# Background matmuls as four column tiles, and one more quad of VectorE exps in the slots of chunks four and five

## The chip, the cores and the metric

The kernel runs on one core of a Trainium2 chip. Five engines work side by side: TensorE (matmuls; PE in the profile, its weight loads PEld), VectorE (DVE), ScalarE (ACT), GpSimd (POOL) and SyncE (SP, which issues the transfers here). The metric is the device time of one execution in microseconds, as the median of several runs; lower is better.

## What is computed

A transformer block for 2048 tokens of 640 features: attention of 32 heads of 20 features after a layer norm, then a gated MLP of 1728 hidden features after another one, each with its residual. All inputs and the output are bfloat16.

```python
def reference(A_x, A_wqkv, A_wo, B_x, B_w_gate, B_w_up, B_w_down):
    def _A_ref(x, wqkv, wo):
        ...
        scores = jnp.einsum("bhqd,bhkd->bhqk", q, k) * (Dh ** -0.5)
        p = _softmax(scores, axis=-1)
        o = jnp.einsum("bhqk,bhkd->bhqd", p, v)
        return (lambda x, *d: x.transpose(*d))(o, 0, 2, 1, 3).reshape(B, S, D) @ wo
    def _B_ref(x, w_gate, w_up, w_down):
        ...
        h = _gelu(g) * u
        return jnp.einsum("bsf,fd->bsd", h, w_down)
    x = A_x
    h = x + _A_ref(_layernorm(x, axis=-1), A_wqkv, A_wo)
    h2 = h + _B_ref(_layernorm(h, axis=-1), B_w_gate, B_w_up, B_w_down)
    return h2
```

`B_x` is not used.

## The kernel before

**Chunks, slots, tiles.** The queries are cut into seven chunks of 512, 512, 256, 256, 256, 128 and 128 rows (`CHUNKS`; chunks four and five are indices 3 and 4). Four heads make a group; a slot is one chunk with so many groups that its accumulator fills 512 columns (1, 2 or 4 groups), which gives 32 slots: 8, 8, 4, 4, 4, 2, 2. A slot has 64 tiles. A tile is the scores of one head for 128 keys in its partitions and 512 columns (a 256-row chunk puts two blocks of keys in a tile, a 128-row chunk four).

**Attention.** A unit (`unit`) is three or two tiles, in turn in the PSUM banks 0 to 2 and 3 to 4. Its score matmuls (L919) use the array as four row tiles of 32 rows, one per head; then one ScalarE activation takes the exp of the whole unit, 1536 or 1024 columns, into the buffers `pts` or `pts2`. The value matmuls (`pv_op`) use the array as four column tiles of 32 columns, with 21 columns of `v_all` each (20 features and a column of ones for the sum of the exps), and accumulate in bank 6. A quad is four tiles, one for each head of the group; its value matmuls are four column tiles at a time, which this document calls a round.

**Exps on VectorE.** `D_QUADS` says how many quads of each slot VectorE takes off ScalarE, by chunk: `(3, 3, 3, 2, 2, 2, 1)`, and none in the first slot. For each tile of such a quad `d_exp` scales the scores from a bank to int16 (L840, 512 columns). After the fourth tile four passes over 2048 columns (`TERMS`) make four shifted bit patterns, whose values, read as bfloat16, sum to the exp up to a common factor. So such a quad has four value quads instead of one.

**Background.** All other matmuls use the whole array of 128 by 128: the projections of keys, queries and values and the output projection (`chain`, L640), gate and up matmuls of the MLP (`mms` in `post`, L1095), and the down matmuls (L1159). In attention they have two PSUM banks, 7 and 5. While the slots of a chunk run, the output projection, norm and MLP of the chunk before (`post`) are to be done. Outside the last chunk gelu is built from five VectorE passes and a ScalarE tanh (`gelu`); gate results leave PSUM by L1131, up results by the product at L1148, down results by the sum at L1163, then an SP transfer writes the output rows. The last chunk (`tail=True`) uses all banks and the Gelu activation.

**The order.** Nothing is ordered by hand. Every operation is recorded with an engine, a planned duration, a priority and what it reads and writes; `Sched.schedule` then makes the order of each engine at build time by a planned clock. Scores have priority 0, values 1, prologue 1.5, epilogues 2, norms 2.5, background 3. Each TensorE operation has a mode, "row", "col" or "full", and a change of mode is planned at 0.098 us. The planner prefers an operation of the present mode unless a score matmul is ready or the first in line has waited for 1.5 us:

```python
if chosen is None:
    chosen, banks = o, got
    if e != "pe" or p[0] < 1 or o.mode == mode[e] or t - o.ready > PE_AGE:
        break
elif o.mode == mode[e]:
    chosen, banks = o, got
    break
```

Where TensorE has nothing to do for long it puts in a dummy matmul (`sc.warm`, a full one of 512 columns, in the profile `ps<-kt_all`). The engines wait for each other by semaphores only; each runs its list strictly in order, and an operation of several matmuls waits at its first and signals at its last.

Of the kernel before, what the change touches and what calls it, by code (L numbers as in the profile page):

```python
# [43 lines left out]
class Sched:  # L44
# [13 lines left out]
    def op(self, eng, fns, dur, prio, reads=(), writes=(), acq=(), rel=(), after=(), sem=None, lat=None, mode=None, util=0.0):  # L58
        if eng == "dve" and rel and prio > self.ev:
            prio = self.ev  # L60
        o = Op()
        o.i = len(self.ops)
        o.eng, o.dur, o.lat, o.sem = eng, dur, DRAIN[eng] if lat is None else lat, sem
        o.util = util
        o.mode = mode
        o.tag = writes[0] if writes else None
        o.fns = fns if isinstance(fns, list) else [fns]
        o.prio = (prio, o.i)
        deps = set(after)
        for r in reads:  # L70
            if r in self.lw:
                deps.add(self.lw[r])
        for w in writes:
            if w in self.lw:
                deps.add(self.lw[w])
            deps.update(self.rd.get(w, ()))
        for r in reads:
            self.rd.setdefault(r, []).append(o.i)
        for w in writes:
            self.lw[w] = o.i  # L80
            self.rd[w] = []
        deps.discard(o.i)
        o.deps = deps
        o.acq = list(acq)
        o.rel = list(rel)
        o.succ = []
        o.ready = 0.0
        self.ops.append(o)
        return o.i

    def schedule(self):
# [11 lines left out]
        mode = {e: None for e in ENGINES}  # L103
# [11 lines left out]
        while done < total:  # L115
# [4 lines left out]
            for e in ENGINES:  # L120
# [53 lines left out]
                if chosen is None:  # L174
                    if e == "pe" and self.warm is not None:
                        while recent and recent[0][0] < t - WARM_WIN:
                            recent.popleft()
                        fb = [b for b in self.warm_banks if owner[b] is None and free_at[b] <= t + 1e-9]
                        free7 = fb and all(hasattr(ops[d], "fin") and ops[d].fin + 0.06 <= t for d in self.warm_deps)
                        if sum(x for _, x in recent) < WARM_MIN * WARM_WIN and (free7 or live):  # L180
                            o = Op()
                            o.i, o.eng, o.lat = len(ops), "pe", DRAIN["pe"]
                            o.prio, o.sem, o.tag, o.util = (9, 0), None, "warm", 0.213
                            o.acq, o.rel, o.succ, o.dur = [], [], [], 0.215
                            if live and (mode[e] == "col" or not free7):
                                o.fns, o.mode, o.deps = list(self.pad), "col", set()
                            else:
                                b = fb[0]
                                o.fns, o.mode = [self.warm[b]], "full"
                                o.deps = set(self.warm_deps) | ({last[b]} if last[b] is not None else set())  # L190
                                last[b] = o.i
                            ops.append(o)
                            chosen = o
                            total += 1
                    if chosen is None:
                        continue
# [126 lines left out]
NTERM = len(TERMS)  # L323
PV_QUADS = 2
PR, PR2 = 12, 4
D_QUADS = (3, 3, 3, 2, 2, 2, 1)
D_QUADS0 = 0
SIX = ()
D_FIRST, D_SPAN = 0, 18
# [8 lines left out]
def bass_sequential_preLN__mha_block__glu_gated_geglu__prompt_kernel(  # L338
# [12 lines left out]
    with ExitStack() as es:  # L351
# [112 lines left out]
        def bank(b, n=512):  # L464
            return PS[:, 512 * b.b:512 * b.b + n]
# [171 lines left out]

        def chain(bk, key, n, steps, reads, prio, acq=True, after=()):
            for k, (l, r) in enumerate(steps):
                yield op("pe", lambda eng, l=l, r=r, k=k: eng.matmul(  # L640
                    bank(bk, n), l, r, start=(k == 0), stop=(k == len(steps) - 1)),
                    c_mm(n), prio, mode="full", util=n / 2400.0, reads=reads, writes=[key], acq=[bk] if (k == 0 and acq) else [],
                    after=after if k == 0 else ())

        def aqk(t):
            return ("xn", t - 3) if t >= 3 else ("aq", t)
# [81 lines left out]
        def q_bound(c, ts, g0, g1, banks, prio):  # L728
            bk = Bank(*banks)
            key = ("bk", sc_id())  # L730
            for k, t in enumerate(ts):
                w_readers.append(op("pe", lambda eng, k=k, t=t: eng.matmul(
                    bank(bk)[0:32, :], sel[:, t, :], aq[t], start=(k == 0), stop=(k == len(ts) - 1)),
                    c_mm(512), prio, mode="full", util=0.05, reads=[aqk(t), ("sel", t)], writes=[key],
                    acq=[bk] if k == 0 else []))
            op("dve", lambda eng: eng.tensor_scalar(qoff[0:32, :], bank(bk)[0:32, :], OFF, None, ALU.add), c_dve(512), prio,
               reads=[key], writes=["qoff"], rel=[bk])
            dma(odr[c], qoff[0:32, :], ("odr", c, g0), ["qoff"], "ow", 2.5, prio, 0.4)
            new = [("qo", c, g0)] + [("q", c, g0, j) for j in range(4)]
            for j in range(4):  # L740
                dma(qt_all[32 * j + 1:32 * j + 21, c, g0:g1, :],
                    qdr[c].rearrange("(g j e) s -> j e g s", j=4, e=DH)[j, :, g0:g1, :], ("q", c, g0, j),
                    [("qdr", c, t) for t in ts] + q_fills[c], f"q{c}{g0}", 2.5, prio, keep=False)
            dma(qt_all[0:128:32, c, g0:g1, :], odr[c].rearrange("(g j) s -> j g s", j=4)[:, g0:g1, :], ("qo", c, g0),
                [("odr", c, g0)] + q_fills[c], f"q{c}{g0}", 2.5, prio, keep=False)
            for g in range(g0, g1):
                q_keys[g][c] += new
# [292 lines left out]
        def post(c, banks, tail):  # L1040
# [48 lines left out]
            def mms(k, w, wkey, after):  # L1089
                bk, key = Bank(*banks), ("bk", sc_id())  # L1090
                for fi in range(min(fn_, NF - k * fn_)):
                    f = k * fn_ + fi
                    for a in range(NA):
                        st = fi == 0 and a == 0
                        op("pe", lambda eng, a=a, f=f, fi=fi: eng.matmul(  # L1095
                            bank(bk)[:, fi * nq:(fi + 1) * nq], w[:, a, F0[f]:F0[f] + 128], hnT[:, a, 128 * tb:128 * tb + nq],
                            start=(a == 0), stop=(a == NA - 1)),
                           c_mm(nq), p, mode="full", util=nq / 2400.0, reads=hk + [(wkey, 0)], writes=[key], acq=[bk] if st else [],
                           after=after if st else ())
                return bk, key  # L1100

# [49 lines left out]
            for tt in range(tb, tb + nt):  # L1151
                t = q0 // 128 + tt - tb
                i = t % 2
                for hf in range(2):
                    bk = Bank(*banks)
                    key = ("bk", sc_id())
                    for f in range(NF):
                        o = hb + f * nq + (tt - tb) * 128
                        op("pe", lambda eng, f=f, o=o, hf=hf, bk=bk: eng.matmul(  # L1159
                            bank(bk, 320), ha_f[:, o:o + 128], wd[:, f, hf * 320:(hf + 1) * 320],  # L1160
                            start=(f == 0), stop=(f == NF - 1)), c_mm(320), p, mode="full", util=0.133, reads=hkeys(f // fn_) + [("wd", 0), "wd2", "wdz"],
                           writes=[key], acq=[bk] if f == 0 else [], after=hdone[-2:] if f == 0 else ())
                    op("dve", lambda eng, bk=bk, tt=tt, hf=hf, i=i: eng.tensor_tensor(  # L1163
                        ob[:, i, hf * 320:(hf + 1) * 320], bank(bk, 320), h_sb[:, tt, hf * 320:(hf + 1) * 320], ALU.add),
                       c_dve(320), p, reads=[key, ("h", tt, hf)], writes=[("ob", i, hf)], rel=[bk], after=first)
                op("sp", I("dma_start", out_hbm[t * 128:(t + 1) * 128, :], ob[:, i, :]), 0.08, p,
                   reads=[("ob", i, 0), ("ob", i, 1)], sem=f"out{i}", lat=2.5)
# [5 lines left out]
        proj_q(0, 0, PRO, P_PRO, "act")  # L1173
        q_bound0(PRO, P_PRO)
        sc.warm_banks = (7, 5, 6)
        sc.warm = {b: I("matmul", PS[:, 512 * b:512 * b + 512], kt_all[:, 0, 0:128], kt_all[:, 0, 0:512], start=True, stop=True,
                        skip_group_check=True) for b in sc.warm_banks}
        sc.pad = [I("matmul", PS[32 * j:32 * j + 32, 512 * 6:512 * 7], zer[:], kt_all[:, 0, 0:512], start=False, stop=False,
                    tile_position=(0, 32 * j), skip_group_check=True) for j in range(4)]
        sc.warm_deps = tuple(sc.lw[kk] for kk in k_keys[0][0])  # L1180
# [75 lines left out]
```

## Time and profile before

| | before |
|---|---|
| time, median of 3 runs | 899.54 us (898.82 to 899.83) |
| the profiled execution: its time | 899.9 us |
| the profiled execution: its span | 898.2 us |
| granted TensorE clock, mean | 0.998 |
| TensorE busy | 836.4 us, 10745 matmuls |
| ScalarE busy | 851.0 us |
| VectorE busy | 689.6 us |
| first exp starts, last exp ends | 35.6 us, 858.9 us |
| last score matmuls start | 857.34 us |

The span goes from the first to the last instruction of one execution; the time has 1.7 us around it. Times within the run are counted from the start of the span. "Busy" of TensorE includes the modelled end of each matmul, which overlaps the next one's start. A row of the chain or timeline gives start, length, engine, line and what was done; x is how many instructions are merged, and brackets give the engine's idle time ahead of it and what ended that.

### The profile page before, as it was taken

The numbers are of one execution on the slowest core, as the hardware profiler recorded it, in microseconds if no ns is written. First come the engines' busy times: TensorE is split into PE (matmuls) and PEld (weight loads), VectorE is DVE, ScalarE is ACT, GpSimd is POOL, SyncE is SP. The second block draws the span as 40 slices with busy tenths as digits, with TensorE's granted clock in tenths as the row PEclk, the third lists the DMA queues.
The fourth block names the chain that finished last, engine by engine and source line by source line (L and its number), as shares of the span: only waits on it lengthen the run. The fifth ranks groups of instructions, "written<-read, shape, count | busy, mean of one in ns | idle before, by whom it ended". The sixth has DMA issues, their size and how long they took to land.

```text
span 898.2 us, 24425 instructions
## 1 busy us (share of the span) xinstructions
PE 836.4 (93%) x10745; PEld 359.1 (40%) x10809; DVE 689.6 (77%) x1263; ACT 851.0 (95%) x777; POOL 75.0 (8%) x147
## 2 busy tenths in 40 slices
PE   3999999899989899999999899999999999999988
PEld 2532222222223222323344333334445446666657
DVE  7839888888989888787778889965669669658553
ACT  6699999999999999999999999999999999999960
POOL 5000000000001100000000100000102000020100
PEclk9999999999999999999999999999999999999999
DMA  7211120222244510000111110011111010031000
GB/s 264 84 50 49 32 67 29 64 81 66 73 137 135 152 46 17 17 14 5 39 51 54 33 34 17 18 30 48 29 54 33 18 48 18 20 63 26 10 17 15
DMA packets 55937, 46.17 MB, mean 51 GB/s; under 512 B 25492, under 2 KB 49392, under 8 KB 55832
## 3 DMA queue, kind: packets, MB, share of 16 engines
q1 hardware_dynamic: 55832, 44.62, 17.8%
q8 instruction: 84, 1.38, 0.6%
q14 instruction: 21, 0.17, 0.1%
HBM read 30.68 MB, written 11.04 MB: 46 GB/s over the span
## 4 chain that ended last, share of the span: by engine, by line
ACT 46%; PE 46%; DVE 6%; issue 1%; DMA 1%; DVEq 0%
ACT pts L359 35%; PE ps L919 14%; PE ps L359 11%; ACT rege L359 10%; PE ps L1095 9%; PE ps L640 6%; PE ps L1159 5%; DVE rege L359 1%; DVE qt_all L359 1%; DVE rege L840 1%; ACT qt_all L359 1%; DVE stats L359 1%; DVE rege L1131 1%; PE ps L585 1%; DMA rege<-xn_t 1%
## 5 line engine op out<-in xcount | busy, mean ns | idle before, releaser
L359 ACT ACTIVATE pts<-ps 128x1536 bf16<-128x1536 f32 x578 | 652.6, 1242 | 10.2 <-PE ps L919 5.7
L919 PE MATMUL ps<-qt_all,kt_all 32*128 32x256 bf16 (+2 forms) x3584 | 320.8, 288 | 25.7 <-ACT pts L359 16.7
L919 PEld LDWEIGHTS ps<-qt_all,kt_all 32*128 32x128 bf16 x3584 | 103.3, 92 | 236.0 <-ACT pts L359 128.3
L840 DVE TENSOR_SCALAR rege<-ps 128x512 int16<-128x512 f32 x200 | 137.0, 687 | 58.6 <-PE ps L919 56.4
L359 ACT ACTIVATE rege<-ps 128x1536 bf16<-128x1536 f32 x115 | 172.1, 1496 | 1.5 <-PE ps L359 0.7
L1095 PE MATMUL ps<-rege,regw 128*128 128x256 bf16 (+2 forms) x951 | 151.6, 289 | 8.4 <-DVE rege L359 2.9
L359 PE MATMUL ps<-pts,v_all 128*21 128x256 bf16 (+2 forms) x2472 | 134.0, 287 | 0.0
L359 PE MATMUL ps<-rege,v_all 128*21 128x512 bf16 (+2 forms) x1564 | 127.6, 312 | 1.3 <-DVE rege L359 1.0
L840 DVE TENSOR_SCALAR qt_all<-ps 128x512 int16<-128x512 f32 x116 | 79.8, 688 | 42.5 <-PE ps L919 40.9
L1095 PEld LDWEIGHTS ps<-rege,regw 128*128 128x128 bf16 x980 | 74.2, 99 | 65.7 <-issue 31.5
L359 POOL TENSOR_TENSOR on<-osb,bsum 128x512 bf16<-128x512 f32 x30 | 42.0, 1399 | 648.2 <-DMA bsum<-rsums 648.1
L359 DVE TENSOR_SCALAR rege<-rege 128x2048 int16<-128x2048 int16 x132 | 92.7, 717 | 2.1 <-PE ps L359 1.2
L640 PE MATMUL ps<-regw 128*128 128x512 bf16 (+1 forms) x340 | 82.0, 349 | 4.6 <-issue 1.7
L1159 PE MATMUL ps<-regw,rege 128*128 128x320 bf16 x448 | 83.7, 302 | 1.1 <-DVE rege L1120 0.5
L359 PEld LDWEIGHTS ps<-pts,v_all 128*21 128x21 bf16 x2472 | 54.3, 91 | 32.4 <-issue 24.4
L359 DVE TENSOR_SCALAR qt_all<-qt_all 128x2048 int16<-128x2048 int16 (+2 forms) x111 | 64.7, 594 | 2.0 <-PE ps L359 1.0
L359 PEld LDWEIGHTS ps<-rege,v_all 128*21 128x21 bf16 x1564 | 41.0, 90 | 45.9 <-issue 23.6
L359 PE MATMUL ps<-qt_all,v_all 128*21 128x256 bf16 (+2 forms) x1048 | 53.7, 282 | 1.7 <-DVE qt_all L359 1.6
L1159 PEld LDWEIGHTS ps<-regw,rege 128*128 128x128 bf16 x448 | 36.6, 97 | 35.8 <-issue 20.1
L359 DVE TENSOR_SCALAR qt_all<-rege 128x2048 int16<-128x2048 int16 x70 | 48.9, 707 | 0.9 <-PE ps L359 0.4
L640 PEld LDWEIGHTS ps<-regw 128*128 128x128 bf16 x360 | 28.9, 98 | 47.5 <-issue 25.0
L1148 DVE TENSOR_TENSOR rege<-rege,ps 128x512 bf16<-128x512 bf16 (+1 forms) x53 | 35.8, 677 | 15.6 <-PE ps L1095 15.4
(98 smaller groups left out, 503.2 us busy)
## 6 DMA issues: line engine op xcount, KB each, us to landing
bsum<-rsums SPq DMA_DIRECT2D x120, 64.0 KB, 2.0
rege<-in_A_x_dram SPq DMA_DIRECT2D x6, 640.0 KB, 5.1
q_rows<-regw SPq DMA_DIRECT2D x20, 128.0 KB, 1.9
out_dram<-rege SPq DMA_DIRECT2D x16, 160.0 KB, 2.2
attn<-on SPq DMA_DIRECT2D x120, 20.0 KB
regw<-in_B_w_gate_dram SPq DMA_DIRECT2D x5, 432.0 KB, 3.3
regw<-in_B_w_up_dram SPq DMA_DIRECT2D x5, 432.0 KB, 3.2
kt_all<-k_rows SPq DMA_DIRECT2D x12, 160.0 KB
```

The lines of the kernel that those rows point to most:

```text
L359: return lambda eng: getattr(eng, method)(*args, **kwargs)
L585: op("pe", lambda eng, a=a: eng.transpose(bank16(bk, D)[:, 128 * a:128 * a + 128], src[:, a * 128:(a + 1) * 128], ident[:]), 0.055, prio, ...
L640: yield op("pe", lambda eng, l=l, r=r, k=k: eng.matmul(bank(bk, n), l, r, start=(k == 0), stop=(k == len(steps) - 1)), c_mm(n), prio, mode ...
L840: d_ops.append(op("dve", lambda eng: eng.tensor_scalar(v[:, 512 * h:512 * h + 512], bank(b), EXP_MUL, -32000.0, ALU.mult, ALU.max), c_dve( ...
L919: return lambda eng: eng.matmul(out()[:, kk * nq:(kk + 1) * nq], kt_all[32 * j:32 * j + 32, g, kt * 128:(kt + 1) * 128], qt_all[32 * j:32 ...
L1095: op("pe", lambda eng, a=a, f=f, fi=fi: eng.matmul(bank(bk)[:, fi * nq:(fi + 1) * nq], w[:, a, F0[f]:F0[f] + 128], hnT[:, a, 128 * tb:128 ...
L1131: op("dve", lambda eng, bg=bg, fv=fv, w=w: eng.tensor_scalar(fv, bank(bg, w), 0.5, None, ALU.mult), c_dve(w), p, reads=[kg], writes=hkeys( ...
L1148: hdone.append(op("dve", lambda eng, bu=bu, fv=fv, w=w: eng.tensor_tensor(fv, fv, bank(bu, w), ALU.mult), c_dve(w), p, reads=[ku] + hkeys( ...
L1159: op("pe", lambda eng, f=f, o=o, hf=hf, bk=bk: eng.matmul(bank(bk, 320), ha_f[:, o:o + 128], wd[:, f, hf * 320:(hf + 1) * 320], start=(f = ...
```

## The change

Two things are changed together. First, a helper `col4` writes one matmul of 128 output partitions as four matmuls of 32 of them, at the column tiles 0, 32, 64 and 96, the tiling that the value matmuls use. `chain`, gate, up and down matmuls and the dummies go through it, and the matmul of `q_bound`, which has 32 columns only, is put at column tile 0. All are planned in mode "col", each at the same planned duration as the full matmul before. Transposes (L585, L1002) and one matmul of the prologue (L752) stay "full". Second, `D_QUADS` becomes 3 instead of 2 for chunks four and five: one more quad in each of eight slots. Since the planner orders everything by these modes and durations, the order on all engines changes.

```diff
@@ Sched.schedule @@
-                                o.fns, o.mode = [self.warm[b]], "full"
+                                o.fns, o.mode = self.warm[b], "col"
...
-D_QUADS = (3, 3, 3, 2, 2, 2, 1)
+D_QUADS = (3, 3, 3, 3, 3, 2, 1)
...
         def chain(bk, key, n, steps, reads, prio, acq=True, after=()):
             for k, (l, r) in enumerate(steps):
-                yield op("pe", lambda eng, l=l, r=r, k=k: eng.matmul(
-                    bank(bk, n), l, r, start=(k == 0), stop=(k == len(steps) - 1)),
-                    c_mm(n), prio, mode="full", util=n / 2400.0, reads=reads, writes=[key], acq=[bk] if (k == 0 and acq) else [],
+                yield op("pe", col4(lambda bk=bk: bank(bk, n), l, r, k == 0, k == len(steps) - 1),
+                    c_mm(n), prio, mode="col", util=n / 2400.0, reads=reads, writes=[key], acq=[bk] if (k == 0 and acq) else [],
                     after=after if k == 0 else ())
+
+        def col4(out, l, r, start, stop):
+            return [lambda eng, j=j: eng.matmul(out()[32 * j:32 * j + 32], l[:, 32 * j:32 * j + 32], r, start=start, stop=stop,
+                                                tile_position=(0, 32 * j), skip_group_check=True) for j in range(4)]
...
@@ q_bound @@
-                    bank(bk)[0:32, :], sel[:, t, :], aq[t], start=(k == 0), stop=(k == len(ts) - 1)),
-                    c_mm(512), prio, mode="full", util=0.05, reads=[aqk(t), ("sel", t)], writes=[key],
+                    bank(bk)[0:32, :], sel[:, t, :], aq[t], start=(k == 0), stop=(k == len(ts) - 1),
+                    tile_position=(0, 0), skip_group_check=True),
+                    c_mm(512), prio, mode="col", util=0.05, reads=[aqk(t), ("sel", t)], writes=[key],
...
@@ mms @@
-                        op("pe", lambda eng, a=a, f=f, fi=fi: eng.matmul(
-                            bank(bk)[:, fi * nq:(fi + 1) * nq], w[:, a, F0[f]:F0[f] + 128], hnT[:, a, 128 * tb:128 * tb + nq],
-                            start=(a == 0), stop=(a == NA - 1)),
-                           c_mm(nq), p, mode="full", util=nq / 2400.0, reads=hk + [(wkey, 0)], writes=[key], acq=[bk] if st else [],
+                        op("pe", col4(lambda fi=fi: bank(bk)[:, fi * nq:(fi + 1) * nq], w[:, a, F0[f]:F0[f] + 128],
+                                      hnT[:, a, 128 * tb:128 * tb + nq], a == 0, a == NA - 1),
+                           c_mm(nq), p, mode="col", util=nq / 2400.0, reads=hk + [(wkey, 0)], writes=[key], acq=[bk] if st else [],
...
@@ post, down matmuls @@
-                        op("pe", lambda eng, f=f, o=o, hf=hf, bk=bk: eng.matmul(
-                            bank(bk, 320), ha_f[:, o:o + 128], wd[:, f, hf * 320:(hf + 1) * 320],
-                            start=(f == 0), stop=(f == NF - 1)), c_mm(320), p, mode="full", util=0.133, reads=hkeys(f // fn_) + [("wd", 0), "wd2", "wdz"],
+                        op("pe", col4(lambda bk=bk: bank(bk, 320), ha_f[:, o:o + 128], wd[:, f, hf * 320:(hf + 1) * 320],
+                                      f == 0, f == NF - 1), c_mm(320), p, mode="col", util=0.133, reads=hkeys(f // fn_) + [("wd", 0), "wd2", "wdz"],
...
-        sc.warm = {b: I("matmul", PS[:, 512 * b:512 * b + 512], kt_all[:, 0, 0:128], kt_all[:, 0, 0:512], start=True, stop=True,
-                        skip_group_check=True) for b in sc.warm_banks}
+        sc.warm = {b: col4(lambda b=b: PS[:, 512 * b:512 * b + 512], kt_all[:, 0, 0:128], kt_all[:, 0, 0:512], True, True)
+                   for b in sc.warm_banks}
```

## The prediction

> **What bounds the kernel now.** I read the page's busy times first, then the stretches of time, the chain that ended last, and the timeline where the change acts.
>
> ```profile
> span 898.2 us, 24425 instructions
> ...
> PE 836.4 (93%) x10745; PEld 359.1 (40%) x10809; DVE 689.6 (77%) x1263; ACT 851.0 (95%) x777; POOL 75.0 (8%) x147
> ```
>
> The two shares do not mean the same. The stretches of time show ScalarE busy for 39.5 to 40.0 us of nearly every 40 us from 50 to 800 us; a busy TensorE includes modelled ends and the drains below. The chain agrees (start, length, what):
>
> ```profile
> 58.26 5.44 ACT pts L359 x5
> 65.04 5.44 ACT pts L359 x5
> ...
> 875.01 6.36 PE ps L1095 x101
> 881.37 3.81 PE ps L1159 x28
> 885.17 5.71 PE ps L1095 x102
> 891.38 3.99 PE ps L1159 x28
> ```
>
> The upper rows stand 6.78 us apart, six exps (three of 1536 columns, three of 1024) or 15 tiles of 512: ScalarE takes 0.452 us per tile and hands on without a gap. The lower rows show that after the last exp (it ends at 858.9) the chain is TensorE's. So there are two stages: attention, paced by ScalarE, and a tail from the last score matmul (857.34) to the end, 40.9 us.
>
> What a change of tiling costs TensorE is seen late in the attention stage (start, busy, what):
>
> ```profile
> 822.10 0.40 PE L359 MATMUL ps<-qt_all,v_all 128*21 128x128 bf16 x16
> 822.33 0.40 PE L359 MATMUL ps<-rege,v_all 128*21 128x128 bf16 x16
> 822.66 0.39 PE L1095 MATMUL ps<-rege,regw 128*128 128x256 bf16 x2
> 822.98 0.40 PE L919 MATMUL ps<-qt_all,kt_all 32*128 32x128 bf16 x12
> ```
>
> Value groups follow each other after 0.23 us: four rounds of four column tiles, 57 ns a round. Before a group of another tiling it is 0.33: 0.10 to 0.11 us per change. Two full matmuls of 256 columns take 0.32, that is 0.21 and the change.
>
> **Part 1, column tiles.** Counting groups in the instruction order of both programs, TensorE changes tiling 1653 times before and 1398 times after: the 233 changes between full and value matmuls fall to 14, while those around score matmuls stay. 255 x 0.11 = 28 us less TensorE work. In attention that lies beside ScalarE's exps and is slack, not time. A round of four column tiles replaces one full matmul of the same columns. The value rows price it at 57 ns for 128 columns; L1095 in the chain above takes 5.71/102 = 56 ns (and 63 in the batch before, after the granted clock had fallen to a mean of 0.93 from 861 to 875). Bounds per round of 128: 56 ns, and 99 ns, the mean of one L1095 LDWEIGHTS in the groups, if a round's four loads hid no better than that; I take 57, since the value rows are the same shape but for 21 stationary columns instead of 32. For 256, 320 and 512 columns the loads have 107 ns or more to hide in.
>
> [...]
>
> **Part 2, one more quad in eight slots.** 32 tiles leave ScalarE (six exps of 1536, seven of 1024): 32 x 0.452 = 14.5 us off the path. TensorE gets three more value quads per slot, 24 x 2 rounds x 0.11 = 5.2 us, hidden in the 28 us above. VectorE gets 32 exps (L840) and 32 term passes (2048 columns). Their pace:
>
> ```profile
> 607.37 1.29 DVE L359 TENSOR_SCALAR qt_all<-qt_all 128x2048 int16<-128x2048 int16 x2
> 608.58 0.69 DVE L359 TENSOR_SCALAR rege<-qt_all 128x2048 int16<-128x2048 int16 x1
> 609.18 0.68 DVE L359 TENSOR_SCALAR qt_all<-qt_all 128x2048 int16<-128x2048 int16 x1
> ```
>
> 0.60 us from start to start, and about the same for L840: 4.8 us per quad, 38.6 us in all. VectorE was busy 27.2 of 29 us at 530 to 559 and 27.8 of 30 at 559 to 589, where chunk four begins. With 4.8 more in slots of 25 us, the evictions of the background no longer fit there.
>
> **What moves because of it.** In the new order all gate and up matmuls of chunk five stand behind the last score matmul; before, only chunks six and seven stood there.
> - TensorE behind the last score: before 30.6 us (280 matmuls of 128 columns, 82 of 320, the rest small); after 51.9 us: 140 rounds of 256 (15.3), 280 of 128 (15.7), 135 of 320 (18.3), value quads, transposes and changes.
> - ScalarE: three tanh of 1024 columns (0.95 from start to start) and one of 512 go with them: 3.3 us. So the last score comes 14.5 + 3.3 = 17.8 us earlier.
> - VectorE: from the last copy to osb on, 29.4 us of work at pace until chunk five's first output half, then little.
> - SP and POOL: chunk five's output DMAs move behind the last score too; DMAs are busy 4 to 7% there and the last output ends it as before. The spread DMAs keep their slots.
>
> **Start.** TensorE has 20.5 us of work ahead of the first score instead of 17.8, since projections now run ahead of transposes: the first exp comes some 2 us later. But it idles 2.69 us for values at 44.27 before, and TensorE's work up to the 20th tile is 27.8 against 28.2 us: -0.4 in sum.
>
> **The tail, before.** Rows of the timeline, with TensorE's idle time in brackets:
>
> ```profile
> 861.13 0.69 DVE L359 COPY osb<-ps 128x512 f32<-128x512 f32 x1
> ...
> 863.42 0.68 PE L1095 MATMUL ps<-rege,regw 128*128 128x128 bf16 x9 [0.79 <-DVE rege L1131]
> 869.00 1.67 PE L359 MATMUL ps<-kt_all 128*128 128x512 bf16 x7 [0.79 <-DVE rege L1131]
> 873.54 0.93 PE L1095 MATMUL ps<-rege,regw 128*128 128x128 bf16 x7 [2.87 <-DVE rege L359]
> ```
>
> 30.6 us of work took 38.0, because the normalisation of chunk seven had nothing beside it (the kt_all rows are dummies) and evictions held up the two background banks. Chunk five now fills that gap. But its MLP needs VectorE longer than TensorE: for 1024 columns of gate and up, four evictions and five passes of about 0.6 or 0.33 us come to 4.9 us, against 40 rounds of 256, 4.4 us. Up to chunk five's outputs the two streams end at T+31.1 (TensorE) and T+2.7+29.4 = T+32.1 (VectorE), with T the last score; they hand banks to each other in order, and I take T+33.7. Then 21.0 us of TensorE work (112 rounds of 320, 103 of 128), 0.6 for the last eviction, as the 0.69 us at 891.38 before, and 2.8 from the last matmul to the end, as before (895.4 to 898.2): T+58.1.
>
> **Sum.** T = 857.3 - 17.8 - 0.4 - 1.5 = 837.6. The 1.5 is from exps that waited for TensorE (of 11.7 us idle before exps in the groups, 5.1 lie behind 48 us), since TensorE's work per tile now stays under ScalarE's. Span 837.6 + 58.1 = 895.7. The run profiled before took 899.9 for a span of 898.2, and the median is 899.54; the span falls by 2.5, so I predict 897.0 us. A difference under 0.2% (1.8 us) can't be told from none here.
>
> **Rivals.**
> - The tail becomes VectorE's: with in-order hand-overs at two banks VectorE gets no denser than before, 10.2 us busy in 861 to 875, 73%. Then the 29.4 us take 40.3, not 31, 9.3 more: 906. It decides once VectorE idles over a seventh of that stretch. For it: three eviction waits before. Against: far more independent work stands there now. 0.24.
> - The tail runs dense (T+56.1) and exps stop waiting (2 us more): 893. For it: each pass takes 0.60 us, under its 0.69 busy. 0.16.
> - Column rounds of 128 take 99 ns: 280 x 42 ns = 12 us, 909. [...] Against: 57 ns with 21 columns. 0.08.
> - VectorE, too full in chunk four, delivers terms late; value matmuls block TensorE in order, and exps idle: 0.6 us per slot over eight slots, 902. Against: exps hardly waited at 559 to 589 (29.86 of 30 us busy). 0.07.
> - Forecast, 894.5 to 900: 0.45.
>
> **How the numbers follow.** Of the forecast, 0.28 lies more than 1.8 us below 899.5 and 0.17 within. Faster: 0.28 + 0.16 = 0.44. Same: 0.17, and 0.02 of the chunk-four rival, 0.19. Slower: 0.24 + 0.08 + 0.05 = 0.37. The range 891 to 907 leaves out the weight-load case and the far ends of the first two rivals. The forecast's own range is 894.5 to 900.
>
> **What would show it.** Right: the last exp ends near 839, about 20 us earlier; no 0.1 us step between value and background rows; behind it a chain of TensorE and VectorE some 17 us longer, with L1095's successor at 57 ns per round. Wrong: rounds of 128 columns above 65 ns, ScalarE idle over 1 us per 40 in chunks four and five, TensorE waits on evictions over 5 us in the tail, or none.

## The result, and the profile after

| | before | after |
|---|---|---|
| time, median | 899.7 us (898.8 to 900.3) | 933.1 us (930.2 to 935.6) |
| the profiled execution: time, span | 899.9, 898.2 us | 935.2, 933.1 us |
| granted TensorE clock, mean | 0.998 | 0.982 |
| last score matmuls start (T) | 857.3 us | 860.8 us |
| from T to the end | 40.9 us | 72.3 us |

The changed kernel takes 1.037 times as long (95% interval 1.033 to 1.041). The forecast was 897.0 us with a range of 891 to 907: the time is outside and has the other sign. Of the 37.4 us by which the span misses the forecast of 895.7, 23.2 lie ahead of T and 14.2 behind it, so the two stages have to be read apart.

Rows of the page after: the head, the clock strip (one of its 40 digits stands for 23 us) and the queue that brings instructions (packets, MB, share of the span of 16 DMA engines). Then the same strip and queue of the page before:

```profile
span 933.1 us, 37145 instructions
...
PE 854.2 (92%) x17106; PEld 383.8 (41%) x17106; DVE 726.0 (78%) x1327; ACT 839.9 (90%) x764; POOL 72.6 (8%) x147
...
PEclk9998999999996999999999999999999999999999
...
q8 instruction: 134, 2.20, 1.0%
```

```profile
PEclk9999999999999999999999999999999999999999
...
q8 instruction: 84, 1.38, 0.6%
```

ScalarE is busy 11 us less and the span is 35 us longer. Two readings lead on. The clock strip has an 8 and a 6 in attention, where every digit of before is a 9. And the queue that brings instructions moved 134 packets, of 16.4 KB each. TensorE's matmuls and loads, 17106 + 17106, are 133.6 times 256 (before, 10745 + 10809 were 84.2 times 256, and the queue moved 84). By these counts a packet is a page of 256 TensorE instructions, and the change needs 50 more of them.

Stretches of attention after: length, then PE, PEld, DVE, ACT and POOL busy with counts, granted clock, DMA share, GB/s. The last row is of the kernel before:

```profile
50.00:100.00 50.00, 47.78 (x608) 15.22 (x605) 30.23 (x55) 46.01 (x41) 1.27 (x1) 0.90 0.15 39
...
150.00:200.00 50.00, 46.28 (x553) 13.06 (x549) 43.03 (x77) 49.98 (x45) 2.77 (x2) 1.00 0.25 71
250.00:300.00 50.00, 44.95 (x488) 12.01 (x480) 35.20 (x61) 41.46 (x37) 3.17 (x3) 0.83 0.44 115
```

```profile
250.00:300.00 50.00, 45.03 (x416) 13.42 (x418) 43.78 (x82) 49.94 (x45) 8.32 (x17) 1.00 0.46 133
```

Where the clock is whole, ScalarE is busy 49.98 of 50 us, as before. Where it is granted at 0.83 or 0.90, ScalarE loses 8.5 and 4 us. The clock records give three halvings (granted clock 0.50), each a whole multiple of 3.41 us: 10.2 us long from 84.5, 6.8 from 135.7 and 17.1 from 279.1, 34 us in all.

The timeline of TensorE around the third one (start, length, what, and in brackets the idle time ahead and its end):

```profile
272.64 0.60 PE L645 MATMUL ps<-kt_all 128*32 128x512 bf16 x8
...
276.20 0.46 PE L645 MATMUL ps<-wo,rege 128*32 128x320 bf16 x8 [1.22 <-DMA rege<-attn]
276.59 0.39 PE L923 MATMUL ps<-qt_all,kt_all 32*128 32x512 bf16 x3
...
278.90 0.33 PE L645 MATMUL ps<-wo,rege 128*32 128x320 bf16 x4 [1.40 <-DVE rege L844]
...
281.59 0.61 PE L923 MATMUL ps<-qt_all,kt_all 32*128 32x512 bf16 x3
```

From 267 to 274 TensorE's background is dummies alone (kt_all). Then TensorE stands 1.22 us for the transfer that brings the attention output, and 1.40 us for a bank that a VectorE exp (L844) still reads. From 279 it runs at half the clock: three score matmuls that took 0.39 us take 0.61, scores come late, and exps wait.

The chain that ended last, in the tail after (start, length, what; "issue" is time in which TensorE waited for nothing that the profile shows):

```profile
891.99 2.50 PE ps L645 x128
894.49 0.97 issue
895.46 2.50 PE ps L645 x128
```

Before, these were 5.71 us of L1095 without a gap. Now groups of exactly 128 matmuls (with their loads 256 instructions, one page) start 3.47 us apart and run 2.50.

What the prediction hoped to see of the tiling changes is there (attention, after):

```profile
600.13 0.40 PE L359 MATMUL ps<-rege,v_all 128*21 128x256 bf16 x8
600.35 0.39 PE L645 MATMUL ps<-rege,regw 128*32 128x512 bf16 x4
600.57 0.39 PE L359 MATMUL ps<-qt_all,v_all 128*21 128x256 bf16 x8
```

Background follows values after 0.22 us, and values follow background after 0.22, which is what two rounds of 256 columns or one of 512 take anyway (0.224 and 0.217 us in 5): the 0.10 us step is gone.

### The profile page after: what moved, and what is told of

It is laid out like the page before. It is cut to its first block, busy times and chain, and to the rows that moved or that the text cites. A ratio compares the mean times of both kernels' runs of the same rounds, so it can differ in the third digit from the quotient of the medians.

```text
span 933.1 us, 37145 instructions
## 1 busy us (share of the span) xinstructions
PE 854.2 (92%) x17106; PEld 383.8 (41%) x17106; DVE 726.0 (78%) x1327; ACT 839.9 (90%) x764; POOL 72.6 (8%) x147
## 4 chain that ended last, share of the span: by engine, by line
PE 46%; ACT 37%; DVE 10%; DMA 3%; issue 2%; POOL 1%; SPq 0%; DVEq 0%; POOLq 0%
ACT pts L359 29%; PE ps L645 21%; PE ps L923 14%; PE ps L359 10%; ACT rege L359 8%; DVE rege L844 2%; DVE qt_all L359 2%; DMA regw<-in_A_wqkv_dram 1%; DVE qt_all L844 1%; DVE rege L359 1%; DMA sums<-osb 1%; ACT qt_all L359 1%; DVE rege L1134 1%; DMA rege<-xn_t 1%; DVE xn_t L359 0%
## 5 line engine op out<-in xcount | busy, mean ns | idle before, releaser
L359 ACT ACTIVATE pts<-ps 128x1024 bf16<-128x1024 f32 (+1 forms) x567 | 643.9, 1251 | 22.4 <-PE ps L923 20.3
L844 DVE TENSOR_SCALAR rege<-ps 128x512 int16<-128x512 f32 x216 | 147.7, 686 | 54.2 <-PE ps L923 50.9
L645 PE MATMUL ps<-rege,regw 128*32 128x256 bf16 (+2 forms) x3920 | 164.2, 289 | 16.4 <-issue 9.3
L844 DVE TENSOR_SCALAR qt_all<-ps 128x512 int16<-128x512 f32 x132 | 90.5, 686 | 32.8 <-PE ps L923 31.4
L645 PEld LDWEIGHTS ps<-rege,regw 128*32 128x32 bf16 x3920 | 83.3, 96 | 57.2 <-issue 28.3
L645 PE MATMUL ps<-regw 128*32 128x512 bf16 (+1 forms) x1440 | 93.4, 357 | 4.7 <-DVE rege L844 2.4
L645 PE MATMUL ps<-regw,rege 128*32 128x320 bf16 x1792 | 83.8, 301 | 3.1 <-issue 1.7
L359 PE MATMUL ps<-qt_all,v_all 128*21 128x256 bf16 (+2 forms) x1216 | 63.6, 282 | 2.0 <-DVE qt_all L359 1.4
L645 PEld LDWEIGHTS ps<-regw,rege 128*32 128x32 bf16 x1792 | 44.5, 96 | 24.5 <-issue 11.7
L645 PEld LDWEIGHTS ps<-regw 128*32 128x32 bf16 x1440 | 34.6, 98 | 44.9 <-issue 18.6
```

The source lines that it names most:

```text
L359: return lambda eng: getattr(eng, method)(*args, **kwargs)
L645: return [lambda eng, j=j: eng.matmul(out()[32 * j:32 * j + 32], l[:, 32 * j:32 * j + 32], r, start=start, stop=stop, tile_position=(0, 32 ...
L844: d_ops.append(op("dve", lambda eng: eng.tensor_scalar(v[:, 512 * h:512 * h + 512], bank(b), EXP_MUL, -32000.0, ALU.mult, ALU.max), c_dve( ...
```

## The experiments

One figure serves throughout, the **waiting of the exps**: from each exp's start to ScalarE's next start, what exceeds 1.333 us (1536 columns) or 0.907 us (1024), summed. It is 21.6 us before and 40.0 after. With it the end of the last exp closes in the profiles to some 0.1 us: the end before (858.9), plus the shift of the first exp, plus the difference in waiting, minus 17.8 where the new `D_QUADS` is used (plus 3.6 in 11, which has a third `D_QUADS`). After: 858.9 + 3.1 + 18.4 - 17.8 = 862.6, and the trace has 862.7.

| kernel | time, us | T | T to end | clock halved ahead of T, us | exps wait, us |
|---|---|---|---|---|---|
| before | 899.7 | 857.3 | 40.9 | 0 | 21.6 |
| after | 933.1 | 860.8 | 72.3 | 34.1 | 40.0 |
| 1: new quads only | 905.7 | 843.8 | 61.1 | 3.4 | 24.4 |
| 2: column tiles only | 922.2 | 871.2 | 49.6 | 23.9 | 32.5 |
| 3: order of after, full matmuls | 929.7 to 948.3 | 878.6 | 59.0 | 30.7 | 58.5 |
| 4: order of before, column tiles | 910.8 | 854.9 | 50.5 | 0 | 17.7 |
| 6: after, full behind T | 918.1 | 858.0 | 59.0 | 27.3 | 35.9 |
| 7: after, more dummies | 922.8 | 853.5 | 68.9 | 17.1 | 32.5 |
| 8: order of before, full behind T | 900.3 | 856.5 | 41.2 | 0 | 19.0 |
| 9: 6, banks planned free later | 925.2 | 851.0 | 70.5 | 17.1 | 30.2 |
| 10: 9, old quads | 908.7 | 868.0 | 40.5 | 17.1 | 28.2 |
| 11: before, last chunk without quad | 892.5 | 860.5 | 31.1 | 3.4 | 21.0 |
| 12: after, two tiles behind T | 919.4 | 856.4 | 59.8 | 23.9 | 35.4 |

Times are medians, for 3 the whole spread; T and what follows are from one profile each. A ratio compares with executions of the kernel before from the same batch, whose medians lie between 899.4 and 900.5 us. The reasons tested first were: the new form of the matmuls lowers the clock; the quads overload VectorE; the new order starves TensorE; and in the tail, rounds are slow.

**1. The quads alone.** In the kernel before:

```diff
-D_QUADS = (3, 3, 3, 2, 2, 2, 1)
+D_QUADS = (3, 3, 3, 3, 3, 2, 1)
```

> The quads alone, with full background matmuls as before. Theory A (the cost is in the form of the background: four times the instructions, of which TensorE gets 256 per 3.4 to 3.5 us, and a lower granted clock for 34 us): no clock loss and no idle time for instructions here; the last score comes some 18 us earlier, the work behind it grows by 24 us, so 896 to 905 us. Rival B (the cost is in the quads: VectorE too full, the MLP of chunk five pushed behind the last score): at least 915 us.

905.7 us, ratio 1.006 (1.004 to 1.007). T comes 13.5 us earlier, and the MLP that is pushed behind it makes the tail 20 us longer. So the second part of the change costs some 5 of the 33 us, and the time is just above the range of theory A. The clock fell only once in attention, for 3.4 us from 84.3: also without column tiles, and at the place of the changed kernel's first halving.

**2. The column tiles alone.** The changed kernel with the old quads:

```diff
-D_QUADS = (3, 3, 3, 3, 3, 2, 1)
+D_QUADS = (3, 3, 3, 2, 2, 2, 1)
```

> The column tiles alone, with the old quads. Theory A: the same clock losses as in the changed kernel, since the order is the same up to chunk three (+15 us), and 280 rounds of 128 columns in the tail at 109 ns instead of 56 (+15 us): 920 to 932 us. Rival B: within 5 us of the kernel before.

922.2 us, ratio 1.024 (1.022 to 1.026), with halvings at 84, 132 and 275, the places of the changed kernel. So the first part makes most of the loss, and the quads are not needed for the halvings.

**3. The order of the changed kernel, its background as full matmuls.** The planner still counts "col", so every engine has the order of the changed kernel:

```diff
         def col4(out, l, r, start, stop):
-            return [lambda eng, j=j: eng.matmul(out()[32 * j:32 * j + 32], l[:, 32 * j:32 * j + 32], r, ...
+            return [lambda eng: eng.matmul(out(), l, r, start=start, stop=stop, skip_group_check=True)]
```

> The order of the changed kernel on every engine, instruction by instruction, but each background round of four column tiles is issued as one full matmul again. Theory A: 895 to 903 us, the clock stays whole and nothing waits for instructions. Rival C (the new order is bad: the planner no longer sees a change of mode and leaves TensorE without work in places, so the clock falls there whatever the form): the clock falls near 84, 135 and 279 us again, 910 us or more. If only the instruction supply counts: 917 to 921.

929.7 to 948.3 us in four executions; the spread allows no ratio, but theory A (895 to 903) falls. The halvings are at 83.5, 138 and 285, at the same places, without one column tile in the background. So the order lowers the clock without the form. Exps wait 58.5 us. This order changes the tiling 1683 times in its trace, 285 more often than the changed kernel, and its plan does not count these; that they are the reason for the longer waiting is likely but not shown.

**4. The order of the kernel before, its background as four column tiles.** The reverse: planned "full", issued through `col4`.

> The order of the kernel before on every engine, but each full background matmul is issued as four column tiles. Theory A: the tail is some 14 us longer for want of instructions, and where the form lowers what the clock is granted by, the clock falls in attention too (+10 us or more): 912 to 930 us. Rival C: the clock stays whole, and the time is 895 to 902 but for what the supply costs, at most 914.

910.8 us, ratio 1.011 (1.009 to 1.014). The profiled execution has no halving in attention; exps wait 3.9 us less than before and T is 2.4 us earlier. (It is the fastest of the four, at 907.1 us with a whole clock. The others have a mean clock of 0.993 to 0.996, against 0.996 to 1.000 for the kernel before in this batch, and no profile, so for them it is not known where the clock fell.) But the tail is 9.6 us longer. With 3, this parts the two: in attention the order harms, and the form helped in this profile; in the tail the form harms.

**5. The rounds by themselves.** The stages of the expectation, one line each: L42 full matmuls, L47 rounds of 128 columns, L52 of 256, L57 of 320, L62 of 512, L67 of 128 columns with 21 stationary ones, and L37 between.

> A kernel of its own that computes nothing of the block: TensorE alone runs long sequences without any wait, 600 full matmuls of 128 columns, then 240 rounds of four column tiles of 32 with 128, with 256 and with 320 columns, 120 rounds with 512, and 240 rounds of 128 columns with 21 instead of 32 stationary columns, with 40 full matmuls of 512 columns between. Theory (instruction supply: 256 TensorE instructions per 3.48 us, eight per round): full ones of 128 columns 56 ns each; rounds of 128 columns 109 ns in the long run in both widths, in bursts at 57 ns with gaps behind them; rounds of 256 columns 109 ns, of 320 about 136 ns, of 512 about 216 ns. Rival (weight loads of 32 columns in turn, about 99 ns a round): no bursts, rounds of 128 columns at 99 ns and more evenly spaced, those with 21 columns at about 65 ns. Rival (the 57 ns of the prediction holds): all rounds at columns/2.4 GHz plus 4 ns, gaps only where an operand is missing, so none.

TensorE's groups (busy, mean ns of one, idle ahead and what ended it), and its timeline:

```profile
L42 PE MATMUL ps<-m,w 128*128 128x128 bf16 x600 | 33.7, 219 | 0.0
...
L52 PE MATMUL ps<-m,w 128*32 128x256 bf16 x960 | 26.8, 273 | 0.1
...
L47 PE MATMUL ps<-m,w 128*32 128x128 bf16 x960 | 16.2, 230 | 10.2 <-issue 10.2
L67 PE MATMUL ps<-m,w 128*21 128x128 bf16 x960 | 14.7, 219 | 9.9 <-issue 9.9
```

```profile
66.11 1.97 PE L47 MATMUL ps<-m,w 128*32 128x128 bf16 x128 [1.54 <-issue]
69.57 1.97 PE L47 MATMUL ps<-m,w 128*32 128x128 bf16 x128 [1.48 <-issue]
...
220.95 1.97 PE L67 MATMUL ps<-m,w 128*21 128x128 bf16 x128 [1.49 <-issue]
```

Busy and idle over 240 rounds: 110 ns a round of 128 columns with 32 stationary ones, 103 with 21 (there the first burst was 227 matmuls long; behind it bursts start 3.45 to 3.73 us apart). Rounds of 256 columns take 112 ns, of 320 take 137, of 512 take 217, full matmuls of 128 columns 56. In the kernel before, full matmuls of 128, 256, 320 and 512 columns follow each other after 56, 109, 136 and 216 ns: 384 more columns in 160 ns, 2.4 per ns. The bursts are of 128 matmuls again, 3.45 to 4.0 us from start to start. Inside a burst 32 rounds take 1.97 us with the modelled end of the last one, some 57 ns each. That is the supply theory in each stage. Weight loads in turn (99 against 65 ns, no bursts) fall, and so does the sustained 57 ns. A column round has eight instructions, so a page holds 256 / 8 = 32 rounds, and 3.45 us or more per page make an estimate of 108 ns or more per round behind the first burst, near the 110 and 112 ns measured with 128 and with 256 columns.

Full matmuls of 128 columns (two instructions per 56 ns) show no idle time (L42); column rounds of 128 (eight instructions) were idle for 10.2 us of 26.4 (L47).

**6. After, with full matmuls behind T.**

```diff
-        def col4(out, l, r, start, stop):
+        def col4(out, l, r, start, stop, full=False):
+            if full:
+                return [lambda eng: eng.matmul(out(), l, r, start=start, stop=stop, skip_group_check=True)]
...
-                                      hnT[:, a, 128 * tb:128 * tb + nq], a == 0, a == NA - 1),
+                                      hnT[:, a, 128 * tb:128 * tb + nq], a == 0, a == NA - 1, full=c >= 4),
...
-                                      f == 0, f == NF - 1), c_mm(320)
+                                      f == 0, f == NF - 1, full=c >= 4), c_mm(320)
```

> The changed kernel with its own order on every engine, but gate, up and down matmuls of chunks five, six and seven (those behind the last score) issued as one full matmul each. Theory (eight instructions per round starve TensorE in the tail): from the start of the last score matmuls to the end 58 us instead of 72.3, the 1 us gaps between pages gone, about 919 us; the halvings of the clock at 84, 135 and 280 stay. Rival (the tail is bound by VectorE's evictions and passes, as the first rival of the prediction): the tail stays at 68 us or more, 929 us or more.

918.1 us, ratio 1.022 (1.018 to 1.026): 15 us less than the changed kernel, 13.3 of them in the tail, 59.0 against 72.3 us. In its chain TensorE runs 26 us without a gap behind the last transposes (the changed kernel has nine gaps of "issue" in its tail, 9.8 us):

```profile
882.30 0.14 issue
882.43 26.03 PE ps L646 x314
```

The rival of a tail bound by VectorE's evictions falls: the same evictions in the same order fit into 59 us.

**7. After, with more dummies.** 179 dummies of 512 columns instead of 83:

```diff
-WARM_WIN, WARM_MIN = 3.4, 0.5
+WARM_WIN, WARM_MIN = 3.4, 0.7
```

> The changed kernel with WARM_MIN at 0.7 instead of 0.5, so that the planner puts in 179 dummies of 512 columns instead of 83; the order of the rest shifts a little. Theory (the clock is halved because the new order leaves TensorE thinly used near 84, 135 and 280): halvings of 7 us or less instead of 34, exps wait 2.5 us or less per 50 there instead of 3.4 to 10.3, the last score starts near 846 instead of 860.9, about 919 us. Rival (the clock falls for another reason, or the dummies take from the scores what the clock gives): 930 us or more.

922.8 us, ratio 1.026 (1.025 to 1.028), between the two expectations. The halvings at 135 and 280 are gone and exps wait 0.9 us between 250 and 300 instead of 10.3. But the one at 85 stays with 10.2 us, and a new one of 6.8 us stands at 177, so 17 us are left where 7 or less were expected. T is 7.3 us earlier.

**8. The order of before, column tiles in attention, full matmuls behind T.** Experiment 4 with the `full` of 6 for chunks six and seven.

> The order of the kernel before on every engine and its D_QUADS; background issued as four column tiles, except gate, up and down matmuls of chunks six and seven (those behind the last score), which stay one full matmul each. Theory (column tiles help TensorE where it has slack of instructions, and cost only in the tail): last score at 855 as with column tiles throughout in this order, 2.4 us earlier than before; from there 41 us to the end, as before; about 897.5 us, a ratio near 0.997. Rival (the 2.4 us earlier is noise of one profile, or the mixed tilings take it back): 899.5 to 902 us.

900.3 us, ratio 1.000 (0.999 to 1.002). The tail is that of before (41.2), T 0.9 us earlier, the first exp 1.7 us later. So column tiles as such are neither gain nor loss here once the tail is spared; the expected 0.3% is not there.

**9. Banks and transfer planned later.** On top of 6, the planner counts a bank that VectorE's exps read free 0.3 us later, and the transfer of the attention output 2.5 us later:

```diff
-                            reads=[("SD", tile)], writes=[vk], rel=[b], after=aft))
+                            reads=[("SD", tile)], writes=[vk], rel=[b], after=aft, lat=0.385))
...
-                   writes=[("hnT", tt) for tt in range(tb, tb + nt)], sem=f"oT{c}", lat=4.5 + nq * 0.002, after=first)
+                   writes=[("hnT", tt) for tt in range(tb, tb + nt)], sem=f"oT{c}", lat=7.0 + nq * 0.002, after=first)
```

> The changed kernel with full matmuls behind the last score (as in the run before this one with its own order), and two planned delays longer: a bank that VectorE's exps read is counted free 0.3 us later, and the transfer that brings the attention output back for the output projection 2.5 us later. So the planner puts background further from the moment at which its bank or its data come. Theory (column tiles let the planner place background at once where it is allowed, in order behind VectorE's exps and that transfer; TensorE stands there, is thinly used, and the clock is halved): TensorE's waits of background matmuls for those exps fall from 9.8 us to 4 or less, the 1.2 to 1.4 us wait for the transfer goes, halvings of 7 us or less instead of 27, the last score starts near 848 instead of 858; the planner leaves 59 instead of 51 us of TensorE work behind it, so about 66 us more, 915 us. Rival (waits at the head of TensorE have nothing to do with it, the background simply runs out at those places): halvings of 17 us or more, last score at 855 or later, 922 us or more.

TensorE's waits from 40 to 860 us (who waited for whom, total, times, longest), first after, then this kernel, then the largest of this kind before:

```profile
PE ps L645 <- DVE rege L844: 6.6, 18, 1.4
...
PE ps L645 <- DVE qt_all L844: 3.2, 6, 1.1
```

```profile
PE ps L647 <- DVE rege L846: 0.6, 2, 0.4
...
PE ps L647 <- DVE qt_all L846: 0.4, 2, 0.2
```

```profile
PE ps L640 <- DVE rege L840: 1.5, 6, 0.4
```

The waits of background for VectorE's exps fall from 9.8 us to 1.0 (0.6 and, into the other buffer, 0.4; the kernel before had 2.5 us in all), that for the transfer is gone, and so are the halvings at 135 and 280. From 250 to 300 the clock is whole and ScalarE busy 49.64 of 50 us:

```profile
250.00:300.00 50.00, 45.77 (x589) 13.82 (x590) 41.99 (x79) 49.64 (x44) 3.71 (x3) 1.00 0.50 132
```

T comes at 851.0, 7 us earlier than in 6 and 3 later than expected. The halving at 85 stays, 10.2 us, and two of 3.4 appear at 389 and 498. The time is 925.2 us, ratio 1.027 (1.026 to 1.029), 7 more than 6: the later plan leaves 59 instead of 51 us of TensorE work behind T, and the tail takes 70.5 us. In time and in halvings (17.1 us) the run lies on the rival's side, T on the theory's. At 280 the waits and the halving went together, as the theory says; the later plan moves other work too, so the waits are not isolated. At 85 the theory does not hold, and the cure costs more than it brings.

**10. The same with the old quads.**

> The same with D_QUADS of the kernel before. Theory: halvings of 7 us or less, the last score near 857, as in the kernel before, instead of 871 with column tiles alone; TensorE has 35 instead of 30 us of work behind it, so some 46 us from there, about 903 us. Rival: halvings of 17 us or more, last score at 865 or later, 911 us or more.

908.7 us, ratio 1.009 (1.007 to 1.011). Halvings of 17.1 us remain (at 86 and 390) and T is 868, not 857. Of the 11 us, 6.6 are exps that wait longer than in the kernel before and 3.9 its later first exp. So the theory failed in all three figures, and the rival is right in two (the time is 2 us under its 911): with the column order even a whole clock at 280 does not bring the attention of before.

**11. The opposite of the second part.** The kernel before with

```diff
-D_QUADS = (3, 3, 3, 2, 2, 2, 1)
+D_QUADS = (3, 3, 3, 2, 2, 2, 0)
```

> The kernel before, its background as full matmuls, with one VectorE quad less in each of the two slots of the last chunk (D_QUADS 3, 3, 3, 2, 2, 2, 0): the opposite of the change's second part. Theory (what counts is how much of the MLPs is left behind the last score): 8 tiles go back to ScalarE, 8 x 0.452 = 3.6 us, so the last score starts near 861; TensorE has 24.2 instead of 30.2 us of work behind it, so 35 instead of 41 us to the end: about 897 us, a ratio of 0.997. Rival (the tail is set by the normalisation of the last chunk and VectorE's evictions, not by TensorE's work left): the tail stays at 40 us or more, 902 us or more.

892.5 us, ratio 0.991 (0.990 to 0.993): faster than both kernels. T is 3.1 us later, against 3.6 expected, and the tail 9.8 us shorter, more than the 6 us of TensorE work that leave it. The other 3.8 were not taken apart; the tail of the kernel before has a halving of 3.4 us, from 873.0, that this one does not have. The end of its chain:

```profile
874.54 1.90 PE ps L1159 x14
876.44 7.83 PE ps L1095 x140
...
884.77 3.99 PE ps L1159 x28
```

From 874.5 on TensorE's only gap in the chain is that of the last product, 0.5 us at 884.3. Before, two batches of some 100 gate and up matmuls stood there with 28 down matmuls between them (the prediction's second fence), and the last matmul ended at 895.4; here 140 are left after chunk six's down matmuls, and the last one ends at 888.8.

**12. Two column tiles of 64 behind T.** Experiment 6, but where it has full matmuls:

```diff
-                return [lambda eng: eng.matmul(out(), l, r, start=start, stop=stop, skip_group_check=True)]
+                return [lambda eng, j=j: eng.matmul(out()[64 * j:64 * j + 64], l[:, 64 * j:64 * j + 64], r, start=start, stop=stop,
+                                                    tile_position=(0, 64 * j), skip_group_check=True) for j in range(2)]
```

> The changed kernel with its own order, but gate, up and down matmuls of chunks five, six and seven as two column tiles of 64 columns each, instead of four of 32 (or one full one, as in an earlier run: 59.0 us behind the last score, 918 us). Theory (instruction supply, 256 instructions per 3.48 us): a round has four instructions instead of eight, so at least 54 ns, about the 56 to 57 ns that 128 columns take anyway; no gaps between pages of the kind that end "issue", from the last score to the end 59 to 62 us, 918 to 922 us. Rival (column tiles themselves, their weight loads or their tiling, are slow behind the last score): rounds of 128 columns stay at 80 ns or more, 65 us or more from the last score to the end, 925 us or more.

919.4 us, ratio 1.023 (1.020 to 1.027), the tail 59.8 us against 59.0 with full matmuls and 72.3 with four tiles. The waits of its tail name no "issue" at all; those of the changed kernel (860 to 933 us) begin with it:

```profile
PE ps L645 <- issue: 9.8, 9, 1.8
```

So it is not column tiling that is slow behind T, but eight instructions in the time of one matmul.

## Why the prediction was wrong, point by point

- **What bounds the kernel now**: right. ScalarE paces attention at 0.452 us per tile wherever the clock is whole, and behind T TensorE ends the chain, before and after.
- **Part 1, fewer tiling changes**: right in mechanism. The 0.10 us step is gone, the trace after has 1398 changes of tiling, as counted, and with only the form changed (4) exps wait 3.9 us less. Only 219 of the 255 changes saved are between full and value matmuls, so those around score matmuls did not quite stay. That most of the 28 us was slack agrees with 8, which is not faster than before.
- **Part 1, the price of a round**: this term failed. 57 ns was read from value rounds in attention, which come a few at a time between other work. In the long run of 5 a round took 110 ns. The bound of 99 ns was the mean of one weight load (L1095, before): the size was near, by luck, and the mechanism wrong, since 5 shows bursts at 57 ns a round with gaps of mostly 1.4 to 2.0 us that end "issue". The rival that rested on it, at 909, got 0.08. By the measured rate the term is 280 x (110 - 57) ns = 14.8 us more; the tails of 6 and of the changed kernel differ by 13.3.
- **Part 2**: the 17.8 us are right. With them the end of the last exp closes to 0.1 us in 1 and in the changed kernel. That chunk five's MLP moves behind T is right too; T to the end in 1 is 61.1 us. The rival of a VectorE too full in chunk four falls: ScalarE was busy for 29.87 of the 30 us from 559 to 589, 29.86 before.
- **Start**: predicted -0.4 us. The first exp came 3.1 us later, the early wait shrank by 2.6: +0.5. (The 2.69 us of idle time at 44.27 are ScalarE's, ahead of an exp, and not TensorE's.)
- **Exps waiting 1.5 us less**: this term failed most. Behind 50 us they waited 21.0 us longer: 9.5 between 250 and 300, 5.7 between 50 and 150, 6.0 behind 500. The prediction looked for a new wait in chunk four and took TensorE's lower work per tile as its only effect on the exps; it left out that the new order leaves TensorE thinly used in places and that its clock was granted at half there, for 34 us. Runs 2 and 3 (23.9 and 30.7 us) show that the order does it, without the quads and without the form. At 280, the largest of the three, the planner, no longer held back by a tiling change, put background close behind the planned release of a bank and the planned end of a transfer, and the real ones came later; TensorE stood there in order with scores behind it. In 9, where these are planned later, this halving is gone. (Over all of attention such waits for VectorE's exps are 9.8 us instead of 2.5.) The other two have another look: in the 3.4 us ahead of 84.5 TensorE waited 0.4 us for an exp of VectorE and had one round of background, where the kernel before had seven full matmuls of 320 columns from 82.2 to 83.7; ahead of 135.7 it had no background from 131.5 to 135.4 at all. There mainly a lack of background, and not a wait for a bank, left TensorE thin; why the planner put none there was not followed up. The one at 135 is gone in 7 and 9. The one near 85 stands in every kernel that has the order planned for column tiles (at 76 in 6), 7 and 9 do not cure it, and 1 has a short one there. The 6.0 us behind 500 are mostly waits of exps for score matmuls; what held these up is open.
- **The tail**: T+58.1 was the sum for rounds at 57 ns. With full matmuls in the same order it is 59.0, and chunk five's first down matmuls start at T+33.7 (891.7 - 858.0), as predicted; with column rounds at T+42.8. So hand-overs and evictions were priced right in sum, with some luck, since the step from T+32.1 to T+33.7 had no row behind it. The rivals "VectorE-bound tail" (906) and "dense tail" (893) both fall.
- **Sum**: 23.2 us ahead of T are 22.5 of waiting and 0.9 of the start, to 0.2 us; the 14.2 behind T are 13.3 of instruction supply and 0.9 of the rest.

## What to carry to other kernels

Before splitting a matmul into tiles, multiply its instructions: at 13.5 ns each (3.45 us per 256 of TensorE's in 5) the eight of a round of four column tiles come to an estimate of 108 ns, and 110 were measured in a long run of 128 columns, against 56 for a full matmul. So here they were nearly free only with 256 columns or more (112 ns in 5, a full matmul of before 109), or in short bursts (57 ns a round). A planner that gets its wish sooner needs true release times, because TensorE, which runs its list in order, turned a planned zero into a wait for all that was queued behind it (1.22 and 1.40 us ahead of 279), and the clock was halved for 17.1 us behind these waits; planning later is no free cure, since it left 8 us more work for the tail (9). And work pushed behind the last step of the pacing engine has to be counted: here a quad more in eight slots brought T 13.5 us forward and made the tail 20 us longer (1), and a quad less at the very end won 0.9% (11).

## What was not expected of the hardware

- TensorE's instructions arrived in pages of 256 (10433 of them in 5, where the queue moved 41 packets), at best one per 3.45 us in 5. Full matmuls of 128 columns with their loads needed a page per 128 x 56 ns = 7.2 us and show no gap (L42).
- The clock was halved here without any long idle stretch. In the 3.41 us (the step of the halvings' lengths) ahead of the halving at 279, matmuls streamed for 0.96 us, and TensorE's longest single wait was 1.40 us. (The streaming is an estimate: the columns of the trace at 2.4 per ns, from the 56 and 216 ns of full matmuls of 128 and 512 columns in the kernel before; a column or row tile is counted as a quarter.) Ahead of 84.5 they streamed for 1.15 us and ahead of 135.7 for 1.29. A low count alone does not decide it: 1.27 us from 204.0 to 207.4 brought no halving, and in 10 neither did 0.96 us from 205.5 to 208.9. In all profiles of this case, each halving in attention from a whole clock follows 3.41 us with 1.29 or less.
